# Attention, soft-MoE and MLP on one core: conversions at other steps, a shorter warm-up, a rearranged end of attention, and g's first part between combine's transposes

## Chip, core and metric

The kernel runs on one core of one Trainium2 chip. The metric is the device time of one execution in microseconds, the median of several runs. TensorE is called PE, VectorE DVE, ScalarE ACT, GpSimd POOL and SyncE SP, as in the profile.

## What is computed

Softmax attention with rotary position embedding over 4 x 8 heads of 576 tokens and 64 channels, then a soft mixture of 8 experts with 4 slots each over the 2304 tokens, then one MLP with SiLU, all in fp32:

```python
q_rot, k_rot = rotate(q), rotate(k)
attn = softmax(q_rot @ k_rot.T / sqrt(64)); x = attn @ v      # (4, 8, 576, 64) -> x (2304, 512)
logits = x @ phi                                              # (2304, 32)
slot_input = softmax(logits, axis=0).T @ x                    # (32, 512), 4 slots an expert
slot_out[e] = relu(slot_input[e] @ w1[e]) @ w2[e]             # 512 -> 1024 -> 512, e = 0..7
x = softmax(logits, axis=1) @ slot_out                        # (2304, 512)
h = x @ w_in; return (h * sigmoid(h)) @ w_out                 # 512 -> 2048 -> 512
```

## The kernel before

The heads are taken in 16 pairs. All of the program up to the MLP's first block stands in an order written by hand: engines take their instructions in the order of the code, and a later part of the MLP is ordered by the scheduler.

**Attention.** A pair p has four steps (idx 1 to 4 of `step`). Each step issues on PE the scores of two chunks of 128 keys (`scores`, L398; the last 64 keys are in `scores_rem`, L411), the products with v (`pv`, L431, L425, L433), and for a later pair the row maxima: the product of L327, a relu (L335 on ACT, L330 on DVE for the fifth block), the product of L343 into the same bank, and on DVE the reduction L348. The bank (tag mx, one buffer) is written again by the next L327 only when the reduction has read it. ACT takes the exponentials (L402). An `evict` on DVE (L442 to L444, 128x320 in step 1, 128x256 in step 3) divides by the sums and frees the bank u.

q and k of a pair are rotated ahead of its turn: `load` brings raw, POOL multiplies with the tables (L277, L274, two of each a pair), DVE adds (L280), ACT copies to hi (L283), DVE takes lo (L286) and the difference of keys kd (L289). The next `load` into the same buffer follows L286.

A table of steps (`at`, `run`) hangs other work between: a task at 10p + 2 idx runs in the middle of step idx of pair p, at 10p + 2 idx + 1 at its end, at 10p + 1 ahead of step 1. Among these are the conversions of w_in (12 blocks, `conv`) and of four blocks of w_out (`conv_o`). The weights arrive as 64-bit words, and `narrow` makes fp32 of them in three instructions: n0 on ACT (L143), n1 on DVE (L146, a shift, 128x512), n2 on DVE (L149, a shift of the low words and an or with n1's result). For w_in a DMA on SP (`keep`, L659, L660) then stores the block. Before, n1 and n2 of w_in come four steps behind n0, the store five; n1 and n2 of w_out come six behind n0.

**End of attention.** The last group of four pairs is taken in two halves (`half`, h0 and h1): logits, their maximum (L569) and exponentials (L578), the transposed weights (`d_t`: products L596, L598, the copy L600), weighted sums of x (`s_mm`, L609, L614), a merge (L617), a copy of the second sums (L623), the slot inputs (`slots`, L625, L629, copy si L630). lt3 (L964) transposes logits that combine needs later. Then layer 1 of the experts begins (L996).

**Combine and MLP.** Combine transposes its weights (`combine_t`, L1079) into banks and copies them to cs (L1086, 128x384). The product of slot outputs and w_in, g, is formed in parts: the first (32 x 128, g0_ps, L1276) and the rest from the stored w_in (L1237, L1254); `split_g` (L1056 on ACT, L1057 on DVE) makes a high and a low part. `hidden` forms a block of the MLP's hidden values from cs and g (L1173, sigmoid L1177, product L1180, high part L1183, low part L1186); `products` adds three products for each of six row tiles (L1266 to L1268) with the high and low parts of w_out (wo_hi L1160 on ACT, wo_lo L1161 on POOL).

## Time and profile before

| | before |
|---|---|
| median of 3 runs | 560.32 us (558.76 to 562.51) |
| profiled execution | 562.48 us |
| its span | 560.7 us |
| PE busy | 542.5 us (97%) |
| DVE busy | 312.7 us (56%) |
| ACT busy | 298.8 us (53%) |
| POOL busy | 112.5 us (20%) |
| mean granted clock | 0.993 |

The profile is of one execution; 1.78 us of its time lie outside its span. A busy PE is not a PE at full speed, since the chip grants a clock, and an engine that sits idle costs nothing unless another waits for it. A row of the timeline gives the start, the duration, the engine, the line, what is written from what with its shape, the count, and in brackets how long the engine sat idle before and what ended that.

### The profile page before, as it was taken

To read this page: it belongs to the slowest core of one execution; us is meant where nothing else is said; L and a number is where in the kernel's file an instruction comes from. 1 tells how busy PE (TensorE), PEld (TensorE's weight loads), DVE (VectorE), ACT (ScalarE), POOL (GpSimd) and SP (SyncE) were. 2 spreads that over 40 slices of the span, in tenths; PEclk is the share of its full clock that TensorE was granted. 3 is DMA by queue.
4 is the path that set the end of the run, shared out by engine and by line. 5 is a ranking of instruction groups with operands and counts; after the bars stand their busy time and mean duration, and the time that the engine had idled before them with its cause. 6 is when DMAs were issued, how large, how long until landed. Compare 5 with 4: busy or idle time off the path is not lost.

```text
span 560.7 us, 15277 instructions
## 1 busy us (share of the span) xinstructions
PE 542.5 (97%) x6283; PEld 437.4 (78%) x6283; DVE 312.7 (56%) x826; ACT 298.8 (53%) x582; POOL 112.5 (20%) x105
## 2 busy tenths in 40 slices
PE   8989999999999999999999989999999999999996
PEld 5668888888888988888862347788888888888885
DVE  4667666676665567654130448877454444644442
ACT  3656666666676566664420346775443444533342
POOL 3475433312333323200000031412000000000000
PEclk9999999999999999999998999999999999999999
DMA  8325777645664675663799885461030000300002
GB/s 330 117 88 196 237 235 264 211 159 173 225 219 147 211 275 180 224 213 92 297 344 365 290 351 191 131 198 63 2 112 1 1 0 0 114 1 1 0 1 112
DMA packets 38720, 89.31 MB, mean 159 GB/s; under 512 B 10598, under 2 KB 13948, under 8 KB 36732
## 3 DMA queue, kind: packets, MB, share of 16 engines
q1 hardware_dynamic: 38652, 88.36, 45.3%
q8 instruction: 49, 0.80, 0.6%
q14 instruction: 19, 0.16, 0.1%
HBM read 78.20 MB, written 7.60 MB: 153 GB/s over the span
## 4 chain that ended last, share of the span: by engine, by line
PE 81%; ACT 7%; DVE 5%; issue 3%; DMA 2%; SPq 1%; ACTq 0%; DVEq 0%
PE ops L1266 11%; PE ops L1268 11%; PE ops L1267 11%; PE u L431 10%; PE st L398 7%; PE psmx L327 3%; PE l L996 3%; PE hps L1173 3%; ACT e L402 3%; PE st_r L411 3%; PE l L1017 3%; PE xps L459 2%; ACT relu L335 2%; PE u L425 2%; PE psmx L343 2%
## 5 line engine op out<-in xcount | busy, mean ns | idle before, releaser
L1180 DVE TENSOR_TENSOR hps<-hps,g 128x384 f32<-128x384 f32 x96 | 50.5, 562 | 81.5 <-ACT g L1177 81.4
L1177 ACT ACTIVATE g<-hps 128x384 f32<-128x384 f32 x96 | 43.2, 489 | 85.0 <-PE hps L1173 84.7
L348 DVE CUSTOM_DVE_ANT_0 relu<-psmx,relu 128x288 f32<-128x288 f32 x142 | 59.4, 454 | 44.7 <-ACT e L402 38.3
L402 ACT ACTIVATE e<-st 128x512 f32<-128x512 f32 (+1 forms) x128 | 76.4, 650 | 10.4 <-PE st L398 10.4
L431 PE MATMUL u<-v,e 128*64 128x65 f32 x2048 | 80.1, 224 | 0.3 <-ACT e L402 0.3
L1266 PE MATMUL ops<-wo_hi,ghi 128*128 128x512 f32 x198 | 77.8, 393 | 0.7 <-ACT ghi L1183 0.7
L1267 PE MATMUL ops<-wo_lo,ghi 128*128 128x512 f32 x198 | 77.4, 391 | 0.3 <-POOL wo_lo L1161 0.3
L1268 PE MATMUL ops<-wo_hi,glo 128*128 128x512 f32 x198 | 77.6, 392 | 0.0
L431 PEld LDWEIGHTS u<-v,e 128*64 128x64 f32 x2048 | 70.9, 137 | 6.7 <-issue 2.6
L335 ACT ACTIVATE relu<-psmx 128x576 f32<-128x576 f32 x63 | 40.9, 651 | 52.5 <-PE psmx L327 40.6
L277 POOL TENSOR_TENSOR raw<-raw,tab 128x576 f32<-128x576 f32 x28 | 40.3, 1439 | 114.4 <-DMA raw<-in_qk_dram 68.3
L1186 DVE TENSOR_TENSOR glo<-hps,ghi 128x384 fp32r<-128x384 f32 x96 | 50.0, 552 | 4.0
L1183 ACT ACTIVATE ghi<-hps 128x384 fp32r<-128x384 f32 x96 | 46.2, 491 | 10.4 <-DVE hps L1180 10.3
L1268 PEld LDWEIGHTS ops<-wo_hi,glo 128*128 128x128 f32 x198 | 37.2, 188 | 8.1 <-DVE glo L1186 0.3
L1266 PEld LDWEIGHTS ops<-wo_hi,ghi 128*128 128x128 f32 x198 | 37.2, 188 | 7.9 <-ACT ghi L1183 0.9
L1267 PEld LDWEIGHTS ops<-wo_lo,ghi 128*128 128x128 f32 x198 | 37.2, 188 | 7.1 <-POOL wo_lo L1161 0.8
L274 POOL TENSOR_TENSOR raw<-raw,tab 128x576 f32<-128x576 f32 x28 | 41.3, 1475 | 0.0
L398 PE MATMUL st<-hi 64*128 64x256 f32 (+1 forms) x256 | 39.3, 301 | 0.0
L398 PE MATMUL st<-hi,lo 64*128 64x256 f32 (+1 forms) x256 | 38.2, 292 | 0.0
L398 PE MATMUL st<-mq,neg_a 64*128 64x256 f32 (+1 forms) x256 | 38.2, 292 | 0.0
L398 PE MATMUL st<-lo,hi 64*128 64x256 f32 (+1 forms) x256 | 38.2, 292 | 0.0
L1266 PE MATMUL ops<-wo_hl,ghi 128*128 128x512 f32 x90 | 35.2, 391 | 0.0
(228 smaller groups left out, 993.5 us busy)
## 6 DMA issues: line engine op xcount, KB each, us to landing
w<-in_w_dram SPq DMA_DIRECT2D x64, 512.0 KB
raw<-in_qk_dram SPq DMA_DIRECT2D x14, 1152.0 KB
w_out_raw<-in_w_out_dram SPq DMA_DIRECT2D x16, 512.0 KB
w_in_raw<-in_w_in_dram SPq DMA_DIRECT2D x12, 512.0 KB
v<-in_v_dram SPq DMA_DIRECT2D x16, 325.0 KB
out_dram<-os SPq DMA_DIRECT2D x18, 256.0 KB
w_in<-w_in SPq DMA_DIRECT2D x8, 256.0 KB
w_in_raw<-in_w_in_dram SPq DMA_DIRECT2D x2, 1024.0 KB
```

The source lines that it names most:

```text
L335: act.activation(out=r, in_=pair[:, :, 0:HS], func=ACTF.Relu)
L348: dve.tensor_tensor_reduce(out=r[:, hd], in0=t[hd], in1=r[:, hd], scale=1.0, scalar=-3.0e38, op0=ALU.add, op1=ALU.max, accum_out=mxs[p % 2 ...
L398: pe.matmul(st[:, hd, 0:n], lhsT=a, rhs=b, start=i == 0, stop=i == 3, skip_group_check=True)
L402: act.activation(out=e[:, :, 0:n], in_=st[:, :, 0:n], func=ACTF.Exp, scale=0.125)
L431: pe.matmul(u[q:q + 64, 2 * i + hd], lhsT=e[:, hd, o:o + 64], rhs=x[:, hd], start=n == 0 and i + hd == 0, stop=n == 4, skip_group_check=True)
L1177: act.activation(out=g[i], in_=t[i], func=ACTF.Sigmoid)
L1180: dve.tensor_tensor(out=t[i], in0=t[i], in1=g[i], op=ALU.mult)
L1183: act.activation(out=ghi[:, i], in_=t[i], func=ACTF.Copy)
L1186: dve.tensor_tensor(out=glo[:, i], in0=t[i], in1=ghi[:, i].bitcast(F32), op=ALU.subtract)
L1266: pe.matmul(t, lhsT=a, rhs=wo_hi[k], start=k == 0, stop=False)
L1267: pe.matmul(t, lhsT=a, rhs=wo_lo[k], start=False, stop=False)
L1268: pe.matmul(t, lhsT=b, rhs=wo_hi[k], start=False, stop=k == 15)
```

## The change

- **Conversions.** n1 and n2 of w_in come six steps behind n0, and the store seven, for 10 of the 12 blocks (where the next block's conversion begins over nine steps later, and for the last). For eight of them this is from ahead of step 1 of a pair to its end, for two from behind step 3 to the end of step 4. n1 and n2 of w_out come three steps behind n0 instead of six: from the end of step 4 to the middle of step 3.
- **Warm-up.** 12 products instead of 14.
- **End of attention.** The copy of the second logits (`keep`) comes ahead of `d_t`, the first half's copy in `d_t` is on ACT, the second half's sums lie in two banks and are copied by ACT and DVE at once, two products whose result nobody reads (`fill_up`) are added, and lt3's transposes come behind the slot products.
- **Combine and MLP.** g's first part is formed between the two parts of combine's last transposes. At the MLP's opening, the conversion of wf_first comes ahead of g's split, the hidden values of block 1 come behind one more row tile of products, and the order written by hand reaches over block 1's rest.

```diff
...
 W_IN_AT = (17, 27, 37, 47, 53, 67, 77, 87, 93, 107, 117, 127)
-W_IN_STEPS = (4, 4, 5)
 FETCH_AHEAD = 5
...
                     if h:
-                        t = ps_mx.tile([128, 2, 512], F32, tag="mx", name=f"dps{i}")[:, 0]
+                        ps["two"] = ps_mx.tile([128, 2, 512], F32, tag="mx", name=f"dps{i}")
+                        t = ps["two"][:, 0]
                     else:
...
                     n = 2 + h
-                    dve.tensor_copy(out=d[:, 0:n], in_=t[:, 0:NSLOT * n].rearrange("p (c s) -> p c s", c=n))
+                    o, i_ = d[:, 0:n], t[:, 0:NSLOT * n].rearrange("p (c s) -> p c s", c=n)
+                    if h:
+                        dve.tensor_copy(out=o, in_=i_)
+                    else:
+                        act.activation(out=o, in_=i_, func=ACTF.Copy)
...
                     t = ps["s"] = (ps_m if h else ps_u).tile([128, DM], F32, tag="m" if h else "u", name=f"sps{i}")
+                    ts = ps["ss2"] = (t, ps["two"][:, 1] if h else t)
                     js = (0, 2, 1, 3) if h else range(4)
...
                         g = 64 * h * (j // 2)
+                        t = ts[j // 2]
                         for c in range(2):
...
                             g = 64 * (j // 2) + 32 * hd
-                            pe.matmul(t[g:g + 32, o:o + 64], lhsT=d[r, 2], rhs=xq[12 + j][r, 8], start=False, stop=True, skip_group_check=True)
+                            pe.matmul(ts[j // 2][g:g + 32, o:o + 64], lhsT=d[r, 2], rhs=xq[12 + j][r, 8], start=False, stop=True, skip_group_check=True)
...
                     t = ps_st.tile([128, 2, 512], F32, tag="st", name="slots")[:, :, 0:2 * NSLOT].rearrange("p b (k s) -> p b k s", k=2)
-                    for r, c in ((slice(0, 64), slice(0, 256)), (slice(64, 128), slice(256, 512))):
-                        act.activation(out=o[r, c], in_=ps["s"][r, c], func=ACTF.Copy)
+                    a, b_ = ps["ss2"]
+                    act.activation(out=o[0:64, 0:256], in_=a[0:64, 0:256], func=ACTF.Copy)
+                    dve.tensor_copy(out=o[64:128, 256:512], in_=b_[64:128, 256:512])
                     for k in range(4):
...
                 at(gc, lambda i=i: conv(i), lambda i=i: cv[i][0]())
+                late_ = W_IN_AT[i + 1:i + 2] > (gc + 9,) or i == 11
                 for j in range(3):
-                    at(gc + W_IN_STEPS[j], lambda i=i, j=j: cv[i][1 + j]())
+                    at(gc + (4, 4, 5)[j] + 2 * late_, lambda i=i, j=j: cv[i][1 + j]())
                 at(gc - FETCH_AHEAD, lambda i=i: fetch(i))
...
                 at(g, lambda k=k: conv_o(k))
-                at(g + 6, lambda k=k: cv["o", k][1](), lambda k=k: cv["o", k][2]())
+                at(g + 3, lambda k=k: cv["o", k][1](), lambda k=k: cv["o", k][2]())
             for i in range(NWA + 5):
...
             clear()
-            warm(14)
+            warm(12)
             for k in (0, 1, 2):
...
             h1[0]((3,))
+            h0[4]()
             h0[5]()
             h1[2]()
-            h0[4]()
+            busy = ps_m.tile([128, 512], F32, tag="m", name="busy0")
+
+            def fill_up(t):
+                pe.matmul(t[:, 0:128], lhsT=ident, rhs=cst_sb[:, 0:128], start=True, stop=True, skip_group_check=True)
+
             h1[3]()
...
             h1[4]()
+            fill_up(busy)
+            h1[6]()
+            busy = ps_u.tile([128, 512], F32, tag="u", name="busy1")
+            h1[7](lambda: None)
+            fill_up(busy)
             t = ps_mx.tile([128, 2, 512], F32, tag="mx", name="lt3_ps")
-
-            def lt3():
-                for i, (o, n) in enumerate(CHUNKS[3]):
-                    pe.transpose(t[0:n, 0, NSLOT * i:NSLOT * i + NSLOT], hb[2][0:32, o:o + n], ident[0:32, 0:32])
-
-            h1[6]()
-            h1[7](lt3)
+            for i, (o, n) in enumerate(CHUNKS[3]):
+                pe.transpose(t[0:n, 0, NSLOT * i:NSLOT * i + NSLOT], hb[2][0:32, o:o + n], ident[0:32, 0:32])
             act.activation(out=lt[:, 15:19], in_=t[:, 0, 0:4 * NSLOT].rearrange("p (c s) -> p c s", c=4), func=ACTF.Copy)
...
-        def combine_t(b):
-            nc_, ch = 5, chs.pop(b)
-            for part in range(2):
+        def combine_t(b, parts=(0, 1)):
+            nc_, ch = 5, chs[b]
+            for part in parts:
                 sel = [i for i in range(nc_) if (i >= 3) == part]
                 o0 = CHUNKS[b][sel[0]][0]
-                t = (ps_h if b > 1 else ps_t).tile([128, 512], F32, tag="h" if b > 1 else "t", name=f"cst{b}_{part}")
+                up = b == 2 or b == 3 and part == 0
+                t = (ps_h if up else ps_t).tile([128, 512], F32, tag="h" if up else "t", name=f"cst{b}_{part}")
                 n = 0
...
         slot_t(1, lambda: combine_t(2))
-        combine_t(3)
-
         gs2 = [spare(10, "gs0")]
+        t = ps_h.tile([128, 512], F32, tag="h", name="g0_ps")[:, 0:128]
+        combine_t(3, (0,))
+        for k in range(4):
+            for r in range(4):
+                pe.matmul(t[32 * r:32 * r + 32], lhsT=so[:, k, :], rhs=w_in_0[:, k], start=k == 0, stop=k == 3, skip_group_check=True)
+        split_g(gs2[0][:, 0:128], t)
+        combine_t(3, (1,))
         order.close()
...
                     f(1)
-                if k + 1 in LATE:
-                    narrow_wo(k + 1)
-                    load_wo(LATE.index(k + 1) + 3)
-                elif k in CONV_AT:
-                    conv_last(CONV_AT.index(k))
+                def ahead():
+                    if k + 1 in LATE:
+                        narrow_wo(k + 1)
+                        load_wo(LATE.index(k + 1) + 3)
+                    elif k in CONV_AT:
+                        conv_last(CONV_AT.index(k))
+
+                if k > 1:
+                    ahead()
                 for f in (f3, f4):
...
                         f(i)
-                if k > 1:
+                if k == 1:
+                    ahead()
+                else:
                     split_hl(k, wf_early[k])
...
-    def g_spread():
+    def g_spread(between):
         t = ps_o.tile([128, 512], F32, tag="o", name="g0_all")[:, 0:384]
...
             pe.matmul(t[:, 96 * r:96 * r + 96], lhsT=sel[0][:, 128 * r:128 * r + 128], rhs=gfull[0], start=True, stop=True)
+        between()
         split_g(gs2[0][:, 128:512], t)
...
     split_hl(0, wf_early[0])
-    t = ps_o.tile([128, 512], F32, tag="o", name="g0_ps")[:, 0:128]
-    for k in range(4):
-        for r in range(4):
-            pe.matmul(t[32 * r:32 * r + 32], lhsT=so[:, k, :], rhs=w_in_0[:, k], start=k == 0, stop=k == 3, skip_group_check=True)
-    split_g(gs2[0][:, 0:128], t)
     hidden(*seq[0], between=g_product)
     products(0, 0, 0, *gt[0, 0])
-    g_spread()
-    for i in (1, 2):
-        products(0, 0, i, *gt[0, 0])
-    for f in n1:
-        f()
+    def first_narrow():
+        for f in n1:
+            f()
+
+    g_spread(first_narrow)
     split_hl(1, wf1)
     gs2.append(spare(4, "gs1"))
-    order.close()
+    for i in (1, 2, 3):
+        products(0, 0, i, *gt[0, 0])
     for i in (2, 3):
...
     later.pop()()
+    order.close()
     extra = {}
...
         for i in range(NI):
-            if (j, k, i) not in ((0, 0, 0), (0, 0, 1), (0, 0, 2)):
+            if n or i > 3:
                 products(j, k, i, ghi, glo)
...
                     f()
-            if i == 2 and n + 2 < len(seq):
+            if i == (2 if n else 4) and n + 2 < len(seq):
                 hidden(*seq[n + 2])
-            elif i == 3 and later:
+            elif i == (3 if n else 5) and later:
                 later.pop()()
...
                 o = g2.tile([128, DM], F32, tag="os", bufs=6, name=f"os{j}_{i}")
```

In this part of the DVE's order (pair 3 of attention; wf_early is w_out's converted block, w_in_1 a block of w_in, kd the difference of keys, psmx the bank of the row maxima) both conversions of the pair stand behind one another, ahead of the relu of L330. Before:

```order
L146 TENSOR_SCALAR wf_early<-hwo_956 128x512
L149 SCALAR_TENSOR_TENSOR wf_early<-w_out_raw_826,wf_early 128x512
L289 TENSOR_TENSOR kd_152<-hi_157 128x288
L146 TENSOR_SCALAR w_in_1_1077<-hw_1078 128x512
L149 SCALAR_TENSOR_TENSOR w_in_1_1077<-w_in_raw_904,w_in_1_1077 128x512
L330 TENSOR_SCALAR relu_154<-psmx_4_1191 128x288
L348 ISA relu_153,mx_155<-psmx_2_1159,relu_153 128x288
```

After (line numbers are one less), the w_out conversion ahead of the eviction of the step before (r, x from the bank u):

```order
L145 TENSOR_SCALAR wf_early<-hwo_952 128x512
L148 SCALAR_TENSOR_TENSOR wf_early<-w_out_raw_824,wf_early 128x512
L441 TENSOR_SCALAR r_0_1072<-u_0_990 128x4
L442 RECIPROCAL r_0_1072<-r_0_1072 128x4
L443 TENSOR_TENSOR x_1071<-u_0_990,r_0_1072 128x256
```

and the w_in conversion between the eviction of 128x320 and the reductions:

```order
L442 RECIPROCAL r_1_1229<-r_1_1229 128x5
L443 TENSOR_TENSOR x_1071<-u_1_1127,r_1_1229 128x320
L145 TENSOR_SCALAR w_in_1_1077<-hw_1078 128x512
L148 SCALAR_TENSOR_TENSOR w_in_1_1077<-w_in_raw_898,w_in_1_1077 128x512
L347 ISA relu_154,mx_155<-psmx_3_1236,relu_154 128x288
L347 ISA mx_155 128x1
```

The w_out block has moved up by one eviction, the w_in block down past the relu, three reductions and the eviction.

On PE at the end of attention, from the first slot products to layer 1 (lt_ps are lt3's transposes, si the slot inputs). Before:

```order
L625 MATMUL slots<-ss,s_b_80 128x32 x4
L964 MATMUL lt_ps<-cst_sb,last_logits 128x32 x4
L964 MATMUL lt_ps<-cst_sb,last_logits 64x32
L629 MATMUL slots<-cst_sb,last_logits 128x32 x4
L996 MATMUL l_0_0_5094<-w_680,si 32x512
```

After (busy is the filler's bank):

```order
L632 MATMUL slots<-ss,s_b_80 128x32 x4
L636 MATMUL slots<-cst_sb,last_logits 128x32 x4
L966 MATMUL busy_4990<-cst_sb 128x128
L980 MATMUL lt_ps<-cst_sb,last_logits 128x32 x4
L980 MATMUL lt_ps<-cst_sb,last_logits 64x32
L1009 MATMUL l_0_0_5096<-w_678,si 32x512
```

The transposes have moved behind both groups of slot products, with a filler ahead of them.

On PE at combine's end, from the last slot outputs' transposes (otp) over combine's last transposes (cst) and g's first part (g_ps) to the first hidden product (hps). Before:

```order
L1033 MATMUL otp_5382<-cst_sb,o_5369 128x128 x4
L1079 MATMUL cst_0_5388<-cst_sb,ch_5346 128x128 x3
L1079 MATMUL cst_1_5393<-cst_sb,ch_5346 128x128
L1079 MATMUL cst_1_5393<-cst_sb,ch_5346 128x64
L1276 MATMUL g_ps<-w_in_90,so 32x128 x16
L1173 MATMUL hps_0_0_5451<-cs_5316,gs_5397 128x384
```

After:

```order
L1046 MATMUL otp_5384<-cst_sb,o_5371 128x128 x4
L1093 MATMUL cst_0_5392<-cst_sb,ch_5348 128x128 x3
L1149 MATMUL g_ps<-w_in_90,so 32x128 x16
L1093 MATMUL cst_1_5415<-cst_sb,ch_5348 128x128
L1093 MATMUL cst_1_5415<-cst_sb,ch_5348 128x64
L1192 MATMUL hps_0_0_5453<-cs_5318,gs_5390 128x384
```

g's first part has moved ahead of the two transposes of the second part.

## Rows read from the trace of the kernel before

**Rows 1.** The page: busy time of PE, share of the span, instructions.
```profile
PE 542.5 (97%) x6283; PEld 437.4 (78%) x6283; DVE 312.7 (56%) x826; ACT 298.8 (53%) x582; POOL 112.5 (20%) x105
```
**Rows 2.** Stretches: length, busy time of each engine, granted clock, DMA share, GB/s.
```profile
292.00:294.00 2.00, 1.61 (x21) 1.40 (x24) 0.36 (x3) 0.61 (x3) 0.00 (x0) 0.73 1.02 390
294.00:296.00 2.00, 2.00 (x12) 0.54 (x16) 0.69 (x4) 0.00 (x0) 0.00 (x0) 0.50 1.04 384
296.00:298.00 2.00, 2.00 (x12) 0.40 (x8) 0.00 (x0) 0.00 (x0) 0.00 (x0) 0.50 1.04 395
298.00:300.00 2.00, 2.00 (x16) 0.51 (x12) 0.00 (x0) 0.00 (x0) 0.00 (x0) 0.56 0.91 305
```
**Rows 3.** Timeline of PE's weight loads: the last of the warm-up.
```profile
6.16 4.05 PEld L858 LDWEIGHTS warm_up<-relu,ones 128*64 128x64 f32 x17 [0.25 <-issue]
```
**Rows 4.** Chain that ended last, end of attention: start, us, what.
```profile
288.04 0.41 DVE mb L569
...
292.36 0.39 PE lt_ps L964 x5
...
293.60 0.30 DVE si L630
```
**Rows 5.** Timeline at combine's end: weight loads of g's first part.
```profile
331.82 0.81 PEld L1276 LDWEIGHTS g_ps<-w_in,so 128*32 128x32 f32 x32 [0.48 <-DVE cs L1086]
```
**Rows 6.** Timeline at the MLP's opening: POOL, DVE and PE's load.
```profile
340.85 1.28 POOL L1161 TENSOR_TENSOR wo_lo<-wf_first,wo_hi 128x512 fp32r<-128x512 f32 x1 [5.08 <-ACT wo_hi L1160]
...
341.00 1.42 DVE L146 TENSOR_SCALAR wf<-hwo 128x512 uint32<-128x512 uint32 x1
...
342.19 0.19 PEld L1267 LDWEIGHTS ops<-wo_lo,ghi 128*128 128x128 f32 x1 [0.78 <-POOL wo_lo L1161]
```
**Rows 7.** Waits of PE in 60 to 280 us: in total, times, longest.
```profile
PE psmx L343 <- DVE relu L330: 1.4, 2, 0.9
```
**Rows 8.** Timeline of DVE and PE at the start of pair 3.
```profile
71.37 0.42 DVE L146 TENSOR_SCALAR w_in<-hw 128x512 uint32<-128x512 uint32 x1
...
71.83 0.69 DVE L149 SCALAR_TENSOR_TENSOR w_in<-w_in_raw,w_in 128x512 uint32<-128x512 uint32 x1
...
72.44 0.45 DVE L330 TENSOR_SCALAR relu<-psmx 128x288 f32<-128x288 f32 x1
...
75.69 0.49 DVE L444 TENSOR_TENSOR x<-u,r 128x320 f32<-128x320 f32 x1
...
76.89 0.46 DVE L348 CUSTOM_DVE_ANT_0 relu<-psmx,relu 128x288 f32<-128x288 f32 x1 [0.71 <-ACT e L402]
...
77.79 0.41 PE L327 MATMUL psmx<-kd,hi 64*128 64x288 f32 x2
```
**Rows 9.** Timeline of POOL and DVE: the rotation's start and the eviction in three pairs.
```profile
75.00 1.42 POOL L277 TENSOR_TENSOR raw<-raw,tab 128x576 f32<-128x576 f32 x1 [6.93 <-DMA raw<-in_qk_dram]
...
90.81 0.49 DVE L444 TENSOR_TENSOR x<-u,r 128x320 f32<-128x320 f32 x1
91.17 1.43 POOL L277 TENSOR_TENSOR raw<-raw,tab 128x576 f32<-128x576 f32 x1 [10.61 <-DMA raw<-in_qk_dram]
...
141.03 0.49 DVE L444 TENSOR_TENSOR x<-u,r 128x320 f32<-128x320 f32 x1
141.62 1.41 POOL L277 TENSOR_TENSOR raw<-raw,tab 128x576 f32<-128x576 f32 x1 [11.36 <-DVE x L444]
```
**Rows 10.** Timeline of POOL and DVE: a subtraction on DVE beside the rotation.
```profile
27.01 1.42 POOL L274 TENSOR_TENSOR raw<-raw,tab 128x576 f32<-128x576 f32 x1
27.61 1.44 DVE L286 TENSOR_TENSOR lo<-raw,hi 128x576 fp32r<-128x576 f32 x1
28.39 1.94 POOL L277 TENSOR_TENSOR raw<-raw,tab 128x576 f32<-128x576 f32 x1
```
**Rows 11.** Timeline of POOL and DVE in step 3 of pair 2.
```profile
63.37 1.41 POOL L274 TENSOR_TENSOR raw<-raw,tab 128x576 f32<-128x576 f32 x1
...
64.81 0.16 DVE L442 TENSOR_SCALAR r<-u 128x4 f32<-128x4 f32 x1 [0.80 <-PE u L425]
```

## The prediction, made before the changed kernel was run

> **What bounds the kernel now.** I read the busy times first: PE is busy 542.5 of 560.7 us [rows 1], so a term counts only where PE waits, or where PE runs at half speed. Then I cut the span into stretches. The granted clock is 1.00 everywhere but in one place, 292 to 300 us, where it falls to 0.50 [rows 2], the 1.2 GHz level. Then the timeline of PE and the waits of PE. There are five places where PE does not run useful work at full speed: the warm-up at the start, a few waits inside attention, the end of attention with the slow stretch behind it, the joint between combine and the MLP, and the MLP's opening. The change has a part in each.
>
> The sum is made against the profiled execution, 562.48 us. That is 2.16 above the median of the runs shown, 560.32; a measurement of this kernel can tell about 1% (5.6 us) from no change.
>
> **Warm-up.** Two matmuls fewer, four PE instructions of the 28 (each product is issued as two passes). The last 17 weight loads take 4.05 us [rows 3], 0.24 each: 4 x 0.24 = **-0.96**. If what stands behind were not ready it would be 0; the product behind follows at once, so I take the whole.
>
> **End of attention.** The chain of waits gives it piece by piece [rows 4]. Before, the copy of d for the first half stands on DVE ahead of the second half's maximum; on ACT it no longer does, and the maximum (0.41 to 0.44 on the chain) can start that much earlier. The transposes of the last logits (0.39) leave the place between the two groups of slot products, but stand now, with a filler product, between these and layer 1's first product, where PE waits anyhow for the copy of si (0.30 and its start, 0.37 in all). The filler ahead of the second s products lies in PE's wait for the copy of dh. With -0.43, -0.39 and then about +0.3 for what the 0.37 does not cover: **-0.5**, between -0.8 and -0.2.
>
> **The slow stretch.** In 292 to 300 us PE loses (1 - clock) x 2 us in each of four rows [rows 2]: 0.54 + 1.00 + 1.00 + 0.88 = 3.4 us of full-speed work. It begins while PE does only the short products of the end of attention and waits between them. The change fills two of these waits and shortens others, so I take it as gone: **-3.4**, with 0 as the other end.
>
> **Combine.** g's first products start at 331.82, behind a wait of 0.48 for the copy of cs [rows 5]; copy, subtraction and the first hidden product follow. In the new order they need only the copy of so and a free bank, and stand ahead of the second part's two transposes too. The wait goes, and two transposes (five take 0.39 in rows 4, so 0.16): 0.48 + 0.16, **-0.65**. The bound is 0, if the copy on ACT, which then comes behind four wo_hi copies, is late by as much.
>
> **MLP opening.** PE waits 0.78 for wo_lo(1) on POOL at 342.19 [rows 6]; DVE's conversion for block 2 beside it takes 1.42 us. The new order converts wf_first ahead of g's split and puts the hidden products behind three more products, so wo_lo(1) is ready some 2.5 us earlier. The wait goes, and something of it returns in the changed order behind: **-0.7**, between -1.3 and +0.5.
>
> These give -0.96 - 0.5 - 0.65 - 0.7 = -2.8, and -6.2 with the slow stretch.
>
> **The conversions in attention.** They decide. The gain first: in all of attention's steady part PE waits for the relu of L330 twice, 1.4 us together [rows 7]. Both times DVE had a w_out and a w_in conversion just ahead of it. They move apart, one up and one down, so **-1.4**.
>
> Now the price. A conversion is two DVE instructions; from one's start to the next's it takes 0.46, and from L149's start to what follows 0.61, 1.07 together [rows 8]. Its new place is behind the eviction of 128x320 and ahead of two reductions L348. There DVE is idle for only 0.71: L348 starts at 76.89, its eviction having been issued at 75.69. The conversion would start at 76.10 (an instruction starts 0.08 before the last one's end, as L330 does at 72.44, so 0.41 behind the eviction's start), and L348 at 77.16, 0.27 late. PE's next L327 at 77.79 writes into the bank which that reduction reads, and follows at once [rows 8], so this is paid on PE, unless something else is in the way.
>
> Something is. In that place POOL does the rotation, four instructions without a gap. It starts at 75.00 in the pair of the rows, at 91.17 and at 141.62 in two others [rows 9], that is 0.7 before to 0.6 after the eviction's start (75.69, 90.81, 141.03). And two kinds of DVE instructions don't run beside POOL. L286 at 27.61 took 1.44, to 0.62 behind the end of POOL's instruction, and POOL's next then took 1.94 instead of 1.42 [rows 10]. L146, the conversion's first half, takes 0.42, but 1.42 at 341.00, to 0.29 behind the end of POOL's (340.85 + 1.28) [rows 6]. Before, all conversions in attention lie where POOL is idle. So each engine waits for the other's whole instruction and comes next at its end. Applied to the pairs, with POOL's spacing of 1.38:
> - POOL in the middle of an instruction (the pair at 75.00, and one like it): L146 ends at 76.38 + 0.29 = 76.67; POOL's next goes, to 78.05; L149 ends 0.6 later, L348 starts at 78.57 in place of 76.89. +1.7, twice.
> - POOL just started (91.17, against 91.22): L146 to 92.84, POOL to 94.22, L149 to 94.8, L348 at 94.74 in place of 92.02. +2.7, once.
> - POOL starts while L146 runs (141.62, against 141.44 to 141.86): POOL to 143.24, L149 to 143.84, L348 at 143.76 in place of 142.23. +1.5, three times.
> - POOL idle: +0.27, twice. The other two of the ten moved blocks fall at a pair's end, where DVE has room.
>
> Together 3.4 + 2.7 + 4.6 + 0.5 = **+11.2**. The low end: if L149 follows L146 before POOL can, the same steps give 0.4 x 2 + 1.5 + 0.27 x 3 + 0.5 = +3.6. No row shows a second DVE instruction of this kind with POOL already waiting; the nearest are those of rows 10, where each time the one that waited came next, so I take the upper end. The Trainium skill (SBUF - State Buffer, "SBUF: two separate sides") says that VectorE and GpSimd share one pair of ports under an exclusive lock, and that whichever starts first keeps it for its whole instruction while the other fully blocks. The trace agrees in rows 6 and 10; by that rule the sum here is the upper one too, as POOL is waiting when L149 comes.
>
> The w_out conversions, four pairs, move to the third step, ahead of the eviction of 128x256. In the first of these DVE waits 0.80 for PE there, and POOL's second of four instructions is running (63.37, to 64.78) [rows 11]; by the same steps the eviction comes up to 2.1 late. In the others POOL is in its last instruction or through. PE needs that eviction's bank later than it needs the reductions'. Between 0 and 5; I take **+1.5**. Behind the later conversions the copies of w_in wait on SP's queue, with a weight load and the next pair's bd behind them; these have more than a step of room: 0.
>
> Attention: -1.4 + 11.2 + 1.5 = +11.3.
>
> **The sum.** 562.48 - 2.8 - 3.4 + 11.3 = **567.6 us**, 1.3% above the median.
>
> **Rivals.**
> 1. L149 follows L146 before POOL: +3.6 in place of 11.2, 560.0 us. For it speaks that no row shows POOL getting in between two such DVE instructions; against it that L149 reads what L146 wrote and starts only behind its end.
> 2. The conversions miss POOL. POOL's start hangs on the landing of raw, which is loaded some 5.5 to 6 us before; if POOL starts over 1.07 us later against the eviction than now, a conversion costs 0.27 in each of eight pairs, 2.2 in all, and w_out none: 562.48 - 2.8 - 3.4 - 1.4 + 2.2 = 557.1, on the other side. Against it: raw is loaded behind the same DVE work as before, and in six of the eight pairs POOL stands where it hurts.
> 3. The reductions' lateness doesn't reach PE: 562.48 - 2.8 - 3.4 - 1.4 = 554.9. Against it stands L327, 0.06 behind the second reduction.
> 4. The clock falls as before, or at another place: +3.4 on any of these, 571.0 on the forecast.
>
> **How the numbers follow.** Forecast 0.5 (with the slow clock in a quarter of it), rival 1 0.18, rival 2 0.24, rival 3 0.08. Slower by over 1% is above 565.9: most of the forecast's case, 0.46. Faster by over 1% is under 554.7: most of rival 3, 0.07. The rest, 0.47. Forecast alone: 564 to 571.5. The range reaches from 556.0, which takes in rival 1 and most of rival 2, to 571.5, the forecast with the slow clock.
>
> **What would show it.** In the changed trace: L146 of w_in behind the eviction at well over 0.42, in the pairs where POOL rotates, and L149 too (over 0.69); POOL's rotation at over 1.42; PE waiting 1.5 us or more for L348 in six pairs of attention, 0.3 in two. No wait for L330. The warm-up of 24 instructions. The clock at 1.00 from 290 to 302. g's first part starting right behind the transposes, no wait for wo_lo(1). I am wrong if L149 starts 0.46 behind L146 beside POOL (rival 1), or if POOL's first instruction starts over a microsecond behind the eviction (rival 2).

## The result

The changed kernel takes 567.6 us, the median of 9 runs (563.6 to 569.0); the kernel before 561.0 (9 runs). The ratio is 1.0108, with a 95% interval from 1.008 to 1.0136: slower, by about 6 us. The profiled execution took 567.65 us with a span of 565.9.

Where the time went shows best as the start of the same instruction in both traces, each read from the timeline of PE:

| first start of | before | after | difference | this part |
|---|---|---|---|---|
| row-maximum product of pair 0 | 10.65 | 9.62 | -1.03 | -1.03 warm-up |
| transposed weights of the last half (dps) | 287.46 | 296.14 | +8.68 | +9.71 attention |
| layer 1's product (l) | 293.95 | 302.10 | +8.15 | -0.53 end of attention |
| last transposes of slot outputs (otp) | 330.19 | 335.48 | +5.29 | -2.86 layer 1 and 2, the slow stretch |
| the MLP's first product | 335.77 | 340.40 | +4.63 | -0.66 combine |
| the MLP's 71st product | 357.00 | 360.80 | +3.80 | -0.83 opening |
| the MLP's last product | 556.10 | 561.03 | +4.93 | +1.13 behind it |

(The 71st product is taken because PE has done the same work ahead of it in both kernels; ahead of the next, the kernel before has formed two more hidden products.) All parts but attention and the last are gains. The waits of PE in attention, from the trace of the changed kernel in the same 60 to 280 us as [rows 7] (in total, times, longest):

```profile
PE psmx L326 <- DVE mx L347: 5.7, 8, 2.2
PE st L397 <- DMA mq<-m: 1.5, 1, 1.5
```

The relu wait of [rows 7] is gone. In its place PE waits for the reductions on DVE, 5.7 us in eight places, and once for a transfer (mq, the row of maxima that the scores need). Why the reductions are late stands in DVE's and POOL's timelines of one pair. DVE first (line numbers are one less than before):

```profile
140.35 0.49 DVE L443 TENSOR_TENSOR x<-u,r 128x320 f32<-128x320 f32 x1
140.76 1.11 DVE L145 TENSOR_SCALAR w_in<-hw 128x512 uint32<-128x512 uint32 x1
141.90 1.78 DVE L148 SCALAR_TENSOR_TENSOR w_in<-w_in_raw,w_in 128x512 uint32<-128x512 uint32 x1
143.60 0.44 DVE L347 CUSTOM_DVE_ANT_0 relu<-psmx,relu 128x288 f32<-128x288 f32 x1
```

POOL and PE in the same stretch:

```profile
140.16 1.43 POOL L276 TENSOR_TENSOR raw<-raw,tab 128x576 f32<-128x576 f32 x1 [9.62 <-DVE r L441]
141.54 1.59 POOL L273 TENSOR_TENSOR raw<-raw,tab 128x576 f32<-128x576 f32 x1
143.09 1.85 POOL L276 TENSOR_TENSOR raw<-raw,tab 128x576 f32<-128x576 f32 x1
```
```profile
144.49 0.40 PE L326 MATMUL psmx<-kd,hi 64*128 64x288 f32 x2 [2.00 <-DVE mx L347]
```

The profile names DVE's r as what ended POOL's wait at 140.16; what POOL reads is raw, whose load was issued at 134.80, 5.4 us before. L145 asks at 140.76 and ends 0.28 behind POOL's first instruction. POOL's second comes next, stretched to 1.59 by that; L148 waits for it and takes 1.78 instead of 0.69; then POOL's third is stretched to 1.85. The reduction starts 3.25 behind the eviction's start instead of 1.20 [rows 8], and PE stands for 2.00. The pair of the eviction at 159.05 goes the same way, with a stall of 2.22; these two are the long ones of the eight.

In another pair nothing meets, and the conversion costs what DVE's time costs:

```profile
89.00 0.49 DVE L443 TENSOR_TENSOR x<-u,r 128x320 f32<-128x320 f32 x1
89.40 0.41 DVE L145 TENSOR_SCALAR w_in<-hw 128x512 uint32<-128x512 uint32 x1
89.85 0.69 DVE L148 SCALAR_TENSOR_TENSOR w_in<-w_in_raw,w_in 128x512 uint32<-128x512 uint32 x1
90.46 0.45 DVE L347 CUSTOM_DVE_ANT_0 relu<-psmx,relu 128x288 f32<-128x288 f32 x1
...
93.97 1.52 DVE L145 TENSOR_SCALAR wf_early<-hwo 128x512 uint32<-128x512 uint32 x1
95.53 1.80 DVE L148 SCALAR_TENSOR_TENSOR wf_early<-w_out_raw,wf_early 128x512 uint32<-128x512 uint32 x1
```

POOL's rotation starts here at 91.04, behind L148's end; the reduction is 0.26 late. The w_out conversion of the same pair then meets it. What an undisturbed w_in conversion costs shows in the stretch ahead, from the eviction at 73.62, with such a conversion behind it, to this one: 15.38, against 15.13 between the same evictions at 75.69 and 90.81 [rows 8, 9]. The stretch behind it, with the meeting of w_out, takes 17.28 instead of 16.39; PE waits there for the eviction of 128x256, for 0.33.

The clock moved too. Stretches of the changed trace (columns as in rows 2):

```profile
140.00:144.00 4.00, 2.49 (x52) 2.15 (x50) 3.90 (x8) 1.63 (x3) 3.84 (x3) 1.00 0.25 99
144.00:148.00 4.00, 3.51 (x38) 3.21 (x40) 1.28 (x8) 2.53 (x5) 2.32 (x2) 0.66 0.56 155
...
160.00:164.00 4.00, 1.78 (x42) 1.61 (x42) 3.32 (x6) 0.72 (x3) 4.00 (x4) 1.00 0.14 52
164.00:168.00 4.00, 4.00 (x74) 3.64 (x72) 2.63 (x10) 3.28 (x7) 1.26 (x1) 1.00 0.71 226
...
236.00:240.00 4.00, 2.46 (x61) 2.18 (x55) 3.17 (x9) 1.87 (x3) 0.00 (x0) 1.00 0.90 316
240.00:244.00 4.00, 3.86 (x31) 2.16 (x31) 0.22 (x1) 1.74 (x3) 0.00 (x0) 0.60 0.45 167
```

The slow stretch of [rows 2] at 292 to 300 is gone, but behind two of the stalls in attention the granted clock falls, to 0.66 and 0.60 in the mean of four microseconds (part of them at the lower level, 1.2 GHz): once behind the stall of 2.00 for a reduction, once behind that of 1.5 for the transfer. Behind the longest stall, 2.22 at 160 to 164, it doesn't. (1 - clock) x 4 gives 1.4 and 1.6, and with the next four microseconds (0.92 and 0.97) 1.7 each. So attention's +9.71 is made up of 5.7 of waits for the reductions, 1.5 of the transfer, 0.7 for two evictions of 128x256 behind w_out's meetings and 3.4 of clock, less the 1.4 of relu waits that are gone: 9.9, which is 0.2 too much.

### The profile page after: what moved, and what is told of

Its sections match the earlier page's. It is cut to its first block, busy times and chain, and to the rows that moved or that the text cites. A ratio compares the mean times of both kernels' runs of the same rounds, so it can differ in the third digit from the quotient of the medians.

```text
span 565.9 us, 15293 instructions
## 1 busy us (share of the span) xinstructions
PE 541.6 (96%) x6283; PEld 438.9 (78%) x6283; DVE 322.8 (57%) x826; ACT 298.9 (53%) x582; POOL 114.0 (20%) x105
## 4 chain that ended last, share of the span: by engine, by line
PE 76%; DVE 8%; ACT 7%; issue 4%; DMA 4%; SPq 0%; ACTq 0%; DVEq 0%
PE ops L1292 11%; PE ops L1294 11%; PE ops L1293 11%; PE u L430 8%; PE st L397 6%; PE psmx L326 3%; PE st_r L410 3%; PE hps L1192 3%; ACT e L401 3%; PE l L1030 3%; PE l L1009 2%; ACT relu L334 2%; PE xps L458 2%; PE u L424 2%; DVE relu L347 2%
## 5 line engine op out<-in xcount | busy, mean ns | idle before, releaser
L276 POOL TENSOR_TENSOR raw<-raw,tab 128x576 f32<-128x576 f32 x28 | 41.4, 1480 | 121.7 <-DMA raw<-in_qk_dram 54.7
L273 POOL TENSOR_TENSOR raw<-raw,tab 128x576 f32<-128x576 f32 x28 | 42.0, 1501 | 0.0
L1294 PE MATMUL ops<-wo_hl,glo 128*128 128x512 f32 x90 | 35.2, 391 | 0.0
```

The lines of the kernel that those rows point to most:

```text
L1294: pe.matmul(t, lhsT=b, rhs=wo_hi[k], start=False, stop=k == 15)
```

## The experiments

Two theories are set against each other. In theory A the price is that DVE's conversion and POOL's rotation wait for one another. In theory B the conversions cost their own time on DVE only, or the loss lies elsewhere. The kernel before took 561.5 to 562.1 in these runs.

**Which move costs: w_in, w_out or neither.** Three kernels from the changed one. Both conversions back:

```diff
-                late_ = W_IN_AT[i + 1:i + 2] > (gc + 9,) or i == 11
+                late_ = False
...
-                at(g + 3, lambda k=k: cv["o", k][1](), lambda k=k: cv["o", k][2]())
+                at(g + 6, lambda k=k: cv["o", k][1](), lambda k=k: cv["o", k][2]())
```

> The changed kernel with the w_in and w_out conversions back at the steps of before; warm-up, end of attention, combine and opening as changed. Theory A (the conversions cost PE about 10 us in attention, by waiting for POOL's instructions and by what follows from it): 557 us, 0.7% under before, within 556 to 559; no PE wait for the row-maximum reductions longer than 0.3 us, the two waits for the relu of 1.4 us in all are back. Theory B (the conversions cost only their own 0.27 each, and the loss sits in the end of attention or the opening): 565 to 567 us.

559.0 us, 0.9964 of before (0.9946 to 0.9982). The loss goes with the conversions; that is A's forecast of 557 but for 2 us, at the upper end of its range (in the profiled run the first row-maximum product started at 11.11, so the shorter warm-up was not felt there). PE's waits have the relu's again and none of over 0.5 for reductions:

```profile
PE psmx L342 <- DVE relu L329: 1.6, 2, 1.1
```

Only w_out's line of that diff (w_in at the new steps):

```diff
-                at(g + 3, lambda k=k: cv["o", k][1](), lambda k=k: cv["o", k][2]())
+                at(g + 6, lambda k=k: cv["o", k][1](), lambda k=k: cv["o", k][2]())
```

> The changed kernel with only the w_out conversions back at their old steps; w_in at the new ones. Theory A: w_in behind the eviction meets POOL in two to six of eight pairs, at 1.5 to 2.7 us each; the two relu waits are gone: 561 to 566 us, DVE's first conversion instruction over 1 us and the second near 1.8 in those pairs, 0.42 and 0.69 in the others. Theory B: w_in at the new steps costs 8 x 0.27 and saves 1.4: within 1 us of the kernel with both at the old steps.

567.0 us (565.9 without one run of 576.7), 1.0078 (1.0051 to 1.0105). The profiled run is a long one, 572.7 us: five of the eight pairs meet POOL in it, and PE waits for reductions in 60 to 280 us:

```profile
PE psmx L326 <- DVE mx L347: 11.4, 7, 2.4
```

Only w_in's line (w_out at the new steps):

```diff
-                late_ = W_IN_AT[i + 1:i + 2] > (gc + 9,) or i == 11
+                late_ = False
```

> The changed kernel with only the w_in conversions back at their old steps; w_out at the new ones. Theory A: w_out meets POOL's rotation in three of four pairs, at 1 to 2 us on the eviction of which PE feels a part; it saves most of the 1.4 us of relu waits: 557 to 560 us. Theory B (w_out is hidden): 555.5 to 556.5 us, the relu waits being saved for nothing.

559.5 us, 0.9962 (0.9944 to 0.998): no different from both back. In the profile attention is 0.65 shorter than with both back. So w_in's move is the price, all of it within the intervals, and w_out's is free in the median although its conversions do meet POOL (up to 1.66 and 1.79 in this profile): what is late behind them, the eviction of 128x256, PE needs later. It waits for none of these evictions here, and for two in the changed kernel, 0.33 each.

**Two blocks alone.** w_out back, and of w_in's blocks only the two with the relu waits at the new step:

```diff
-                late_ = W_IN_AT[i + 1:i + 2] > (gc + 9,) or i == 11
+                late_ = gc in (27, 117)
```

> As the kernel with all conversions at the old steps, but the two w_in blocks that come right behind a w_out conversion (those with the relu waits) six steps behind instead of four. Theory A: POOL starts behind these two in the changed trace (0.8 and 1.5 us behind the conversion's end), so they cost 0.27 each and save 1.4: 0.9 us under the kernel with all at the old steps, near 556 us; if POOL now comes earlier, 2 to 3 us over it. Theory B: 0.9 under it as well, so this run tells of the size of the saving, not between the theories.

564.1 us, 1.004 (1.0023 to 1.0056), 5.1 over the kernel with all blocks back. The gain that I reckoned with did not come: in this run POOL started 0.23 behind the one eviction and 0.14 ahead of the other, and both conversions met it. DVE, then POOL, at the first:

```profile
74.11 1.53 DVE L145 TENSOR_SCALAR w_in<-hw 128x512 uint32<-128x512 uint32 x1
75.68 1.77 DVE L148 SCALAR_TENSOR_TENSOR w_in<-w_in_raw,w_in 128x512 uint32<-128x512 uint32 x1
```
```profile
73.94 1.43 POOL L276 TENSOR_TENSOR raw<-raw,tab 128x576 f32<-128x576 f32 x1 [6.79 <-DMA raw<-in_qk_dram]
75.32 1.58 POOL L273 TENSOR_TENSOR raw<-raw,tab 128x576 f32<-128x576 f32 x1
76.86 1.84 POOL L276 TENSOR_TENSOR raw<-raw,tab 128x576 f32<-128x576 f32 x1
```

Of these two pairs, that between the evictions at 73.71 and 92.80 took 19.1 us instead of 15.1, that between 223.78 and 243.76 20.0 instead of 16.4: 3.6 to 4.0 each, 2.4 and 2.1 of them stall and the rest a slow stretch behind it.

**POOL taken away.** The rotation's products on POOL cut to 8 of 576 columns, once with the new steps and once with the old (f0 is shown, f1 has the same line):

```diff
                 def f0(i, eng=pool, w=slice(0, S)):
+                    w = slice(0, 8) if eng is pool else w
```

> The changed kernel, all conversions at the new steps, with POOL's part of the rotation cut to 8 of 576 columns (q and k of pairs 2 and up stay unrotated, so the output is another); POOL's four instructions are then short, every other instruction is as in the changed kernel. Theory A (the price is DVE's and POOL's waiting for one another): no conversion instruction is over 0.9 us, the reductions are 0.27 late, PE waits 0.2 to 0.3 for them eight times, the relu waits are gone: 557 to 560 us. Theory B (the price is DVE's time or the order of transfers): 565 to 568 us, PE still waiting 2 us for reductions.

> The same cut of POOL's rotation in the kernel with all conversions at the old steps: what POOL's absence does by itself. Theory A: nothing to gain in attention but up to 0.5 us at DVE's other two-operand instructions that meet POOL, 557.5 to 559 us, within 1.5 us of the one with the new steps. Theory B: 558.5 to 559.5 us, 7 us under the one with the new steps.

559.1 us (0.9962, 0.994 to 0.9983) with the new steps, 557.6 (0.9936, 0.9912 to 0.9961) with the old. With POOL out of the way, the changed kernel loses 8.5 us of its 567.6, and the conversions run at their own time (groups of DVE in 55 to 275 us, the idle time ahead at the end):

```profile
L148 DVE SCALAR_TENSOR_TENSOR w_in<-w_in_raw,w_in 128x512 uint32<-128x512 uint32 x12 | 8.3, 696 | 0.4
L145 DVE TENSOR_SCALAR w_in<-hw 128x512 uint32<-128x512 uint32 x12 | 5.0, 417 | 0.0
```

In the changed kernel these means are 873 and 550. This decides for A: same order, same transfers, same work on DVE, and only POOL's duration differs. What POOL's absence gives by itself, with the old steps, is 1.4 us (557.6 against 559.0), so it isn't that which takes the loss away. The intervals of the two kernels overlap; in the profiles, attention is 0.52 longer with the new steps. That is what B had right: seven waits of 0.22 to 0.26 for the reductions, less the 0.9 of relu waits that the old steps have.

**One operand instead of two.** Both halves of the conversion as shifts of one strided operand, for attention's blocks of w_in and w_out (the two halves are no longer put together; what the two instructions become there, other blocks keep the old ones):

```diff
-            dve.tensor_scalar(out=o, in0=hi, scalar1=3, scalar2=None, op0=ALU.logical_shift_left)
+            dve.tensor_scalar(out=o, in0=words[:, :, 1], scalar1=3, scalar2=None, op0=ALU.logical_shift_left)
...
-            dve.scalar_tensor_tensor(out=o, in0=words[:, :, 0], scalar=29, in1=o, op0=ALU.logical_shift_right, op1=ALU.bitwise_or)
+            dve.tensor_scalar(out=o, in0=words[:, :, 0], scalar1=29, scalar2=None, op0=ALU.logical_shift_right)
```

> The changed kernel, all conversions at the new steps, but in attention both halves of each conversion are shifts of one strided operand of the raw words (the result of w_in and four blocks of w_out is wrong); DVE has as many instructions, at about 0.4 to 0.7 us each. Theory A (the price is the waiting of two instructions for POOL, not DVE's time): the two instructions do not wait for POOL, no reduction is more than 0.6 us late, PE has no wait over 0.7 us for them, 558 to 561 us. Theory B (DVE's time at that place, or the order of DMAs, is what costs): as the changed kernel, 566 to 568 us.

565.3 us (1.0048, 1.0019 to 1.0076). This run alone did not separate the theories. I had supposed that a strided operand would keep the instruction from waiting for POOL; it does not. Alone each half of a w_in block took 0.41 to 0.43, beside POOL up to 1.43 and 1.51. It adds one thing: in the four pairs of eight where POOL was out of the way the reduction started 1.20 behind the eviction, as before, so two DVE instructions of 0.4 are free there. In the other four PE stood for 1.7 to 2.1, and the kernel was 5 to 6 us over that with both conversions back.

**The late transfer.** The eleventh block of w_in back at its old steps:

```diff
-                late_ = W_IN_AT[i + 1:i + 2] > (gc + 9,) or i == 11
+                late_ = (W_IN_AT[i + 1:i + 2] > (gc + 9,) or i == 11) and i != 10
```

> The changed kernel with one w_in block, the eleventh, back at its old steps, four and five behind its first instruction. In the changed trace a weight load on SP waits 3.4 us for this block's stored copy, the row of negative maxima is issued behind it, and PE waits 1.5 us for that and then has a slow stretch of 1.7 us. If that is the cause, these 3.2 us go in the profile, and the median falls by 1 to 3 us, to 564.5 to 566.5; the relu wait of that pair is back with 0.5. If the late w_in block is not the cause, the wait for the maxima stays and the time is within 0.5 us of 567.6.

566.3 us (1.0099, 1.0066 to 1.0131). Its interval overlaps that of the changed kernel (1.008 to 1.0136), so the median does not show the gain; the profile does. The wait for mq is gone from it, that pair takes 16.4 instead of 20.0, and attention is 3.1 shorter, with the same two meetings as in the changed trace. So the cause is the one that SP's waits named there, a weight load that waits for the store of this block, with mq's copy behind it on the queue:

```profile
SPq L128 <- DMA w_in<-w_in: 3.4, 1, 3.4
```

**The fillers.** Both conversions back, and without the two filler products:

```diff
-            busy = ps_m.tile([128, 512], F32, tag="m", name="busy0")
...
             h1[4]()
-            fill_up(busy)
             h1[6]()
-            busy = ps_u.tile([128, 512], F32, tag="u", name="busy1")
             h1[7](lambda: None)
-            fill_up(busy)
```

> The kernel with all conversions at the old steps and the rest as changed, without the two filler products at the end of attention. If the fillers are what keeps the clock up behind the end of attention, the slow stretch of before is back in the profile there, and the time is 2 to 3 us over the same kernel with fillers (559.0): 561 to 562. If the shorter waits of the new order do it, the clock stays at 1.00 and the time is 559.0 less up to 0.4, as the second filler lies on PE's path.

558.7 us (0.9939, 0.992 to 0.9959), the same as with fillers within the intervals. The stretch from dps to layer 1 is 5.51 instead of 5.96. No slow stretch follows at the end of attention in this profile:

```profile
292.00:296.00 4.00, 3.64 (x67) 2.92 (x63) 1.57 (x4) 1.36 (x5) 0.00 (x0) 1.00 1.03 388
296.00:300.00 4.00, 3.99 (x43) 1.49 (x45) 1.05 (x6) 0.35 (x2) 0.00 (x0) 1.00 1.05 393
```

The profiled run itself took 562.0 us, 3.2 over the median. The old steps stall in it as well: PE waits 2.09 for the relu, where [rows 7] has 0.9 at most, and a slow stretch of 1.7 follows (granted clock 0.83 and 0.74 in 220 to 228 us).

```profile
221.80 0.40 PE L342 MATMUL psmx<-hi,bd 128*128 128x288 f32 x1 [2.09 <-DVE relu L329]
```

**Two versions meant to be better.** Without fillers, w_in back, w_out at the new steps; and the same with the MLP's opening in its old order, whose core is:

```diff
-    g_spread(first_narrow)
+    g_spread()
+    for i in (1, 2):
+        products(0, 0, i, *gt[0, 0])
+    for f in n1:
+        f()
     split_hl(1, wf1)
     gs2.append(spare(4, "gs1"))
-    for i in (1, 2, 3):
-        products(0, 0, i, *gt[0, 0])
```

> A version meant to be better: w_in at the old steps, w_out at the new ones, no filler products, the rest as changed. From the profiles: w_out at the new steps gave 0.65 in attention, the fillers cost 0.45 at its end and the clock does not need them: 557.9 to 558.5 us, 0.5 to 1 under the kernel with all conversions at the old steps (559.0). If w_out meets POOL in other pairs, 559 to 561.

> The same with the MLP's opening in the order of before, g's first part still between combine's transposes. In the changed profile the opening gains 1.0 us up to the 72nd product and loses 1.35 behind it, where conversions wait for POOL. If that loss belongs to the new order, the profile shows neither, and the median is 0.3 us under the same kernel with the new opening; if it is chance of the run, it is 1.0 us over.

559.7 (0.9971, 0.9953 to 0.9988) and 561.4 (0.9991, 0.9969 to 1.0013). Neither beats the two kernels at 558.7 and 559.0. In the first profile the slow stretch is there again, without fillers:

```profile
292.00:296.00 4.00, 4.00 (x28) 1.27 (x30) 0.99 (x6) 0.35 (x2) 0.00 (x0) 0.59 1.05 394
```

The second has the loss behind the 71st product too (1.41, against 1.17 in the first), so it doesn't belong to the new order. From the MLP's first product to its last the first takes 220.62 in its profile and the second 221.26: there the new opening is worth 0.6. The medians, 1.7 apart, have intervals that overlap.

## The prediction, point by point

The total was forecast at 567.6 and measured at 567.6. That is better than the steps were, and in part luck: attention came out at +9.71 instead of +11.3, the slow stretch at -2.86 instead of -3.4, the opening with what stands behind it at +0.30 instead of -0.7, and these errors offset one another. The forecast also starts from a profiled run of 562.48, above the median of 561.0.

**The mechanism was right.** DVE and POOL take turns by whole instructions, and POOL goes between L146 and L149 (L145 and L148 after). Every meeting of a w_in conversion in these traces, but for the run with other instructions, shows it, 1.1 to 1.5 for the first and 1.77 or 1.78 for the second. Rival 1, by which the second follows at once, is out. The rule of the Trainium skill (SBUF - State Buffer, "SBUF: two separate sides") says that the other engine blocks for the whole instruction, and the rows at 140 to 145 us agree. That the waiting one comes next is shown by the order POOL, DVE, POOL, DVE in these rows.

**The count was wrong.** The prediction has six of eight pairs meeting POOL. In the changed profile two did: in the pairs of 75.00 and 91.17 [rows 9] POOL started 1.34 and 2.04 behind the eviction instead of 0.69 ahead and 0.36 behind. The step that failed is "applied to the pairs": I took each pair's distance from POOL's start to the eviction from one trace of before. But the change itself moves the eviction (it comes 4.2 behind DVE's last L285 at the first, where it was 6.3 behind L286), and the landing of raw moves by itself: it is loaded at 83.47 for the start at 91.04, 7.6 us later, where 5 to 6 was usual. With w_in alone five pairs met, with two blocks alone both. So rival 2 was true for four of the six pairs in this run. A number of meetings that changes from run to run would also account for the 5 us over which the runs of the changed kernel spread; only one of them has a profile, so that isn't shown.

**Three terms were missing or wrong**, and the first two stand where the four meetings would have. First, a stall can bring a slow stretch behind it, 1.7 us, twice in the changed profile; rival 4 named it as a possibility, the sum did not have it. Stalls of PE of 1.7 to 2.4 us for the reductions occur fifteen times in the profiles with w_in blocks at the new steps; behind seven the clock falls to the lower level for 1.7 us' worth, behind eight it doesn't, and the longest without (2.2) is longer than the shortest with (2.0). Their length doesn't decide it, and what does stays open. Second, the transfers behind the late store: I put them at 0, and once it was 1.5 us. The part read wrongly is "more than a step of room": I looked at what stands behind the store on SP, and not at the weight load that needs the store's buffer. Third, the opening: -0.83 up to the 71st product (forecast -0.7), then +1.13, so +0.30 in all. (The wait of 0.78 from which I took the 0.7 is that of the weight loads; PE itself stood for 0.35 there.) Behind the 71st product DVE's conversions meet POOL's wo_lo just as in attention (DVE, POOL and PE of the changed trace):

```profile
359.00 1.34 POOL L1180 TENSOR_TENSOR wo_lo<-wf,wo_hi 128x512 fp32r<-128x512 f32 x1 [1.63 <-ACT wo_hi L1179]
```
```profile
359.23 1.67 DVE L148 SCALAR_TENSOR_TENSOR wf<-w_out_raw,wf 128x512 uint32<-128x512 uint32 x1
360.81 1.02 DVE L1199 TENSOR_TENSOR hps<-hps,g 128x384 f32<-128x384 f32 x2
```
```profile
361.99 0.50 PE L1292 MATMUL ops<-wo_hi,ghi 128*128 128x512 f32 x1 [0.57 <-ACT ghi L1202]
...
363.72 0.44 PE L1192 MATMUL hps<-cs,gs 128*128 128x384 f32 x1 [0.70 <-DVE glo L1205]
```

The conversion holds up the hidden values behind it on DVE, and PE waits for their high part, then for the low part. The two waits stand in all twelve profiles of kernels with a part of the change (0.57 to 0.81, and 0.70), and not in that of before, so they aren't chance; since the kernel with the old opening has them as well, what brings them was not settled.

**Sizes.** Warm-up -0.96, measured -1.03 here; in the other eleven profiles the same start lies at 9.54 to 10.22, and once, with both conversions back, at 11.11, against 10.65 before. End of attention -0.5, measured -0.53, but before it has a microsecond at the lower clock in it [rows 2] and after it has none: in the two kernels with POOL cut, where the clock falls ahead of layer 1, the new order with its fillers takes 6.43 and 6.51, no less than before (6.48). So how much of the 0.53 is order and how much clock isn't separated; without fillers it takes 5.51 to 5.63. Slow stretch -3.4, measured -2.86 from layer 1 on. Combine -0.65, measured -0.66. A meeting: 1.5 to 2.7, measured 2.0 to 2.4 of stall. w_out: +1.5, measured -0.65 of attention in one profile and nothing in the median. The relu waits belong to w_in, which stood right ahead of the relu: with w_out alone moved they stay at 1.3 us, with w_in alone 0.3 is left. The slow stretch at the end of attention is not a matter of the fillers alone: it was there in a profile without them and absent in another without them, and three of nine profiles with them have it or a part of it (34.5 to 36.0 us from layer 1 to otp, instead of 33.4). What decides it stays open.

## What to carry over

Before a DVE instruction on SBUF is moved, look at what POOL does at the new place, in the same trace and in its neighbours: with shared turns a pair of 1.1 us ends 2.9 to 3.3 us behind its start (from 140.76 to 143.68 in the rows above). Two instructions in a row wait twice, because the other engine comes between. And where the other engine's start hangs on a transfer, read its spread, not one distance: a place that is free in one run is not free in the next.

## What was not expected of the hardware

A DVE shift with a single strided operand (128x512) runs in 0.42 us and waits for POOL like the one on contiguous data. A stall of PE of about 2 us was followed by a stretch at the lower clock in seven cases of fifteen (0.66 in the mean of 144 to 148 us), and by none in the others (160 to 168 us). Loads of raw, all of one size, let POOL start 5.4 us behind their issue in one pair (134.80 to 140.16) and 7.7 behind it in another (189.37 to 197.03).
